# Dynamic convolution and tanh-shrink MLP: the load of the output weights is handed to the queue ahead of block 1's GpSimd products instead of behind two of them

## The chip, the cores and the metric

The kernel runs on one core of one Trainium2 chip. The metric is device time in microseconds (us) for one execution, and the median over runs is compared. The engines are named as in the profile: PE is TensorE's matmul, PEld its weight load, DVE is VectorE, ACT is ScalarE, POOL is GpSimd, SP is SyncE. SPq and POOLq are the instruction streams from which SP and POOL hand transfers to the 16 DMA engines; in the profile's list of DMA queues, q1 (hardware_dynamic) carries SP's transfers and q0 (software_dynamic) POOL's.

## The reference

Two steps. The first is a causal convolution over 7 positions whose weights differ for every token and head (softmax over the 7 taps); the second is a two-layer MLP with h - tanh(h) between.

```python
w = exp(weight_gen - max);  w = w / (sum(w) + 1e-09)        # B, S, 8 heads, 7 taps
x_pad = concatenate([zeros(B, 6, D), x], axis=1)            # B=8, S=4096, D=192
x_unf = x_pad[:, arange(S)[:, None] + arange(7)]            # B, S, 7, 192
y = einsum('bshk,bskhg->bshg', w, x_unf)                    # 24 channels a head
h = y.reshape(32768, 192) @ w_in                            # 192 x 2048
out = (h - tanh(h)) @ w_out                                 # 2048 x 192
```

## The kernel before

The 32,768 tokens are cut into 32 blocks of 1024. For each block the work goes through five stages.

1. SP loads x (with a halo of 6 earlier positions, into a ring of four places, `load_x`) and weight_gen (`load_wg`). ACT takes the exponential, DVE sums and scales.
2. The seven tap products, x times the tap's weight, are formed with `tap_product` (L299), in the steady state almost wholly on POOL. The products lie in the tiles `pa` (taps 0 to 3) and `pb` (taps 4 to 6). Some of them are added up by accumulating transfers that POOL issues (`dma_sum`, L288).
3. PE transposes the products with identity matmuls and adds the remaining ones up in PSUM (`conv_sums`, L526); ACT copies the result to `convT`.
4. The first matmul (`gemm1`, L586) makes 16 f tiles of 128 hidden channels from `convT` and `w_in`; for each, ACT forms tanh (L599) and DVE subtracts (L600) into `gt`. Three PSUM buffers rotate, so the matmul of f tile k waits for the subtraction of f tile k-3.
5. The second matmul (`out_stream`, L655) multiplies `gt` by `w_out`; ACT copies the result to `out_sb` (L674), and SP stores a whole block.

The instruction order on each engine is written out by hand; nothing reorders it. Each engine works through its own list, and waits stand where an operand has to be ready. In the steady state the second matmul of block n-1 runs between the f tiles of block n, and POOL forms the products of block n+2.

The change lies in the ramp, the first 37 us, where blocks 0 and 1 are prepared. Weights come in through POOL's queue, as these transfers also convert from fp32 to bf16. `load_w_in` (L747) brings f tiles 0 to 6 first, into the lower 64 partitions; ACT copies them to the upper 64 (L814). `rest_of_w_in` issues the second part, f tiles 7 to 15, behind block 0's last POOL product; as soon as it has landed, SP issues a transfer that copies it to the upper 64 partitions (L822). SP's queue then holds x of block 2 (L174) and a weight_gen tile (L163). `load_w_out` (L741) brings all of w_out. It is called from a hook in `products(1)`: the function goes through a list of tap products (engine, first tap, last tap plus one, token range) and calls a hook right behind the product whose first tap is the hook's key.

```python
TAPS1 = ((True, 0, 1, 0, 8), (True, 1, 2, 0, 8), (False, 4, 6, 0, 8), (False, 6, 7, 0, 8), (False, 2, 4, 0, 8))
...
        hooks={} if WOUT_CAST else {6: load_w_out},
```

`True` stands for DVE, `False` for POOL. With the key 6, POOL's list reads: second part of w_in, taps 4 and 5 of block 1 (one product), tap 6, w_out, taps 2 and 3, and then the first products of block 2, which wait for that block's x.

Of the kernel before, what the change touches and what calls it, by code (L numbers as in the profile page):

```python
# [16 lines left out]
def kernel(  # L17
# [61 lines left out]
    X3_BEHIND = None  # L79
    HALF = ()  # L80
    STORE_BEHIND = tuple(range(5, 31))
    WOUT_CAST = ()
    SKEW = 6
    TAPS1 = ((True, 0, 1, 0, 8), (True, 1, 2, 0, 8), (False, 4, 6, 0, 8), (False, 6, 7, 0, 8), (False, 2, 4, 0, 8))
# [57 lines left out]
    pace_of = {}  # L142
    sum_of = {}
    second = {}

    def order(inst, other, reason):
        tc.add_manual_dep(
            inst.ins,
            other.ins.name,
            mybir.DependencyInfo(mybir.DependencyClass.Sync, mybir.DependencyReason.DATA),  # L150
            reason=reason,
        )
# [3 lines left out]
    def tokens(t, n):  # L156

        m = n // 2
        return t[2 * m * TOK : 2 * (m + 1) * TOK].rearrange("(p s j) ... -> p s j ...", p=P, j=J)[:, n % 2]
# [127 lines left out]
    def dma_sum(out, in_):  # L287
        return nc.gpsimd.dma_start(  # L288
            out=out.rearrange("p k j d -> p k (j d)"),
            in_=in_.rearrange("p k j d -> p k (j d)"),  # L290
            accum_op=mybir.AluOpType.add,
            max_dma_last_dim=2 * J * D,
        )
# [65 lines left out]
    def products(n, taps=None, sums=None, hooks={}):  # L359
# [6 lines left out]
        pa = held[n][2] if n in held else papool.tile([P, KA, J, D], BF16, name="pa")  # L366
# [5 lines left out]
        else:  # L372
            if n in PB2:
                pb = npool.tile([P, K - KA, J, D], BF16, name="pb2", tag="spare")
            else:
                pb = pbpool.tile([P, K - KA, J, D], BF16, name="pb")
# [7 lines left out]
        def mul(eng, k0, k1, j0=0, j1=J):  # L384
            w = wsm_v if eng is nc.vector else wsm[:]
            return tap_product(eng, prod(k0, k1), x_t, w[:, j0:j1, :, k0:k1], (1, K), k0, k1, j0, j1)

        def parts(*ks):
            return [[prod(k, k + 1)[:, 0] for k in ks]] * NC
# [18 lines left out]
        def most(k0, k1):  # L408
            return mul(nc.gpsimd, k0, k1, 0, left[k0])
# [16 lines left out]
        def rest():  # L426
            a = PART_FILL.get(n, 0)
            if n in PART:
                if a:
                    mul(nc.gpsimd, KA, K, 0, a)  # L430
                dma_sum(pa[:, 0:2], pa[:, 2:4])
                if n + 1 in SCALE_EARLY:
                    prescale(n + 1)
            if n - 1 in whole:
                mul(nc.gpsimd, KA, K - 1)
                third_sum(n - 1)
                mul(nc.gpsimd, K - 1, K)
            else:
                mul(nc.gpsimd, KA, K, a, J)
            if n in PART:  # L440
                prods_of[n] = parts(4, 5, 6, 0, 1)
            else:
                def first_sum():
                    dma = dma_sum(pa[:, 0:3], pb[:, 0:3])
                    if n in LOCKED:
                        order(dma, last_sub[0], "place of the transfer")

                if n in LAST_TAP and n in SUM_BEHIND:
                    most(KA - 1, KA)
                    first_sum()  # L450
                elif n in SUM_LATE:
                    sum_of[n] = first_sum
                else:
                    a = min(FILL.get(n, 0), left[KA - 1]) if n in LAST_TAP else 0
                    if a:
                        mul(nc.gpsimd, KA - 1, KA, 0, a)
                    first_sum()
                    if n + 1 in SCALE_EARLY:
                        prescale(n + 1)
                    if n in LAST_TAP and a < left[KA - 1]:  # L460
                        mul(nc.gpsimd, KA - 1, KA, a, left[KA - 1])
                if n in TWO_SUMS:
                    to_sum[n] = pa
                    prods_of[n] = parts(0, 1)
                elif n in HALF:
                    to_sum[n] = pa
                    prods_of[n] = parts(3, 1, 0)
                else:
                    prods_of[n] = parts(3, 0, 1, 2)
                if n == NTOT - 1:  # L470
                    second_sum(n)
                    third_sum(n)
# [3 lines left out]
    def prescale(n):  # L476

        wsm, wsm_v, e_t, zr = wsm_of[n]
        scale(nc.gpsimd, wsm[:], e_t, zr[:])
        wsm_of[n] = (wsm, wsm_v, None, None)  # L480

    def second_sum(n):

        if n in to_sum:
            pa = to_sum.pop(n)
            pairs = 1 if n in HALF else 2
            second[n] = dma_sum(pa[:, 0:pairs], pa[:, 2 : 2 + pairs])
            if n in THREE or n in SINGLE:
                whole[n] = pa

    def third_sum(n):

        if n in whole:
            pa = whole[n]
            dma_sum(pa[:, 0:1], pa[:, 1:2])
            if n in SINGLE:
                whole.pop(n)
                prods_of[n] = [[pa[:, 0]]] * NC
# [142 lines left out]
    def out_stream():  # L641

        for i in range(LAST + 1):
            ops = []
            for r, blk in ((0, i), (1, i - 1)):
                if not 0 <= blk < LAST:
                    continue
                n, j = divmod(blk, J)
                if r == 0:
                    half[blk] = obank[blk % 2]  # L650
                ops.append((r, n, j, half[blk]))
            for f in range(NFT):
                for r, n, j, po in ops:
                    col = (j % 2) * HT + (j // 2) * P
                    mm = nc.tensor.matmul(  # L655
                        po[:, 0:D],
                        lhsT=g_of[n][f][r * R : (r + 1) * R, col : col + P],
                        rhs=w_out[r * R : (r + 1) * R, f, :],
                        start=(r == 0 and f == 0),
                        stop=(r == 1 and f == NFT - 1),  # L660
                    )
                    if r == 1 and f == 0 and i in (1, LAST):
                        order(mm, probe[0] if i == 1 else last_act[0], "row tiles in one bank")
                if f == NFT - 1 and i > 0:
                    store_out(i - 1)
                yield

    def store_out(blk):
        n, j = divmod(blk, J)
        po = half.pop(blk)  # L670
        if j == 0:
            out_of[n] = opool.tile([P, J, D], FP32, name="out_sb")
        out_sb = out_of[n]
        last_act[0] = nc.scalar.activation(out=out_sb[:, j, :], in_=po[:, 0:D], func=ACT.Copy)  # L674
        if j == J - 1:
            out_of.pop(n)
            g_of.pop(n)
            dma = nc.sync.dma_start(
                out=tokens(out, n),
                in_=out_sb[:],  # L680
            )
            if n in STORE_BEHIND and n + 3 in second:
                order(dma, second[n + 3], "order of the transfers")

    pairs = out_stream()

# [89 lines left out]
    def soft1():  # L776
# [17 lines left out]
        hooks={1: rest_of_w_in} | ({SOFT1_AT: soft1} if SOFT1_AT else {}),  # L794
# [24 lines left out]
    if SOFT_EARLY:  # L819
# [4 lines left out]
        1,  # L824
        taps=[(V if v else G_, k0, k1, j0, j1) for v, k0, k1, j0, j1 in TAPS1],
        sums=SUMS1,
        hooks={} if WOUT_CAST else {6: load_w_out},
    )
    conv(0, (0, 1), (2,))
    if not SOFT_EARLY:  # L830
# [200 lines left out]
```

## Time and profile before

| what | value |
|---|---|
| median of 3 runs | 735.81 us (735.81 to 737.36) |
| the profiled execution's own time | 735.9 us |
| its span, first to last instruction | 734.1 us |
| granted TensorE clock | 1.00 |
| PE busy | 715.7 us (97%) |
| DVE busy | 681.0 us (93%) |
| POOL busy | 660.6 us (90%) |
| ACT busy | 636.3 us (87%) |
| load of w_out, issue to landing | 9.9 us |
| second part of w_in, issue to landing | 5.2 us |

Times in the timelines are microseconds from the first instruction: start, length, engine, line, operation, output and inputs, count, and in brackets the idle time before it with what ended it. "w_out<-in_moe_w_out_dram" is a transfer by the names of its tiles. A DMA issue on SPq or POOL is the time in which the engine hands the transfer over; the transfer itself runs later. In the view by stretches the columns are length, busy time and count for PE, PEld, DVE, ACT, POOL, then the granted clock, the mean busy share of the 16 DMA engines and GB/s.

### The profile page before, as it was taken

How to read it: one execution, taken by the hardware profiler on the slowest of the kernel's cores; microseconds unless marked ns; L12 is line 12 of the kernel's file. 1: busy time of each engine (PE TensorE's matmuls, PEld its weight loads, DVE VectorE, ACT ScalarE, POOL GpSimd, SP SyncE). 2: the span in 40 equal slices, each digit the busy share in tenths (PEclk: the TensorE clock that was granted, in tenths of full speed). 3: DMA queues.
4: the chain of work that ended last, by engine and by line, in shares of the span. 5: the costliest groups of instructions: out<-in, count | busy, mean ns of one | idle time of the engine just before them, and what ended most of it. 6: DMA issues, size and time to landing. Idle time of an engine off the chain costs nothing.

```text
span 734.1 us, 29774 instructions
## 1 busy us (share of the span) xinstructions
PE 715.7 (97%) x13472; PEld 549.6 (75%) x13472; DVE 681.0 (93%) x718; ACT 636.3 (87%) x871; POOL 660.6 (90%) x170
## 2 busy tenths in 40 slices
PE   3899999999999999999999999999999999999998
PEld 2477877777777777777777777777777777777777
DVE  7999999999999999999999999999999999988883
ACT  4888888888889899999898998998998989888982
POOL 7999999999999999999999999999999999996000
PEclk9999999999999999999999999999999999999999
DMA  7745266664558787877888877787887878676412
GB/s 206 162 102 163 102 175 157 185 167 113 142 144 217 153 221 184 180 202 172 212 172 205 203 157 206 178 194 187 216 172 171 209 172 208 164 153 136 105 46 88
DMA packets 35053, 122.97 MB, mean 168 GB/s; under 512 B 4607, under 2 KB 9455, under 8 KB 33006
## 3 DMA queue, kind: packets, MB, share of 16 engines
q0 software_dynamic: 20208, 53.48, 42.4%
q1 hardware_dynamic: 14718, 67.59, 25.8%
q8 instruction: 105, 1.72, 0.9%
q14 instruction: 22, 0.18, 0.1%
HBM read 45.08 MB, written 25.17 MB: 96 GB/s over the span
## 4 chain that ended last, share of the span: by engine, by line
PE 94%; DVE 4%; ACT 1%; issue 0%; DMA 0%; DVEq 0%
PE obank L655 45%; PE ph L586 44%; PE pc L526 4%; DVE gt L600 2%; PE po L701 1%; DVE pa L299 1%; DVE pb L299 0%; DMA wg_t<-in_weight_gen_dram 0%; ACT th L599 0%; DVE obank L258 0%; DVE zsum L218 0%; DVE wsm L281 0%; ACT wg_t L204 0%; DVE obank L281 0%; ACT convT L544 0%
## 5 line engine op out<-in xcount | busy, mean ns | idle before, releaser
L600 DVE TENSOR_TENSOR gt<-ph,th 128x1024 bf16<-128x1024 f32 x512 | 598.6, 1218 | 32.2 <-ACT th L599 25.9
L599 ACT ACTIVATE th<-ph 128x1024 f32<-128x1024 f32 x512 | 513.0, 1027 | 65.5 <-PE ph L586 51.0
L586 PE MATMUL ph<-convT,w_in 64*128 64x512 bf16 x3072 | 412.9, 377 | 4.6 <-DVE gt L600 3.6
L655 PEld LDWEIGHTS <-gt 64*128 64x128 bf16 x7936 | 352.7, 94 | 84.4 <-issue 12.1
L655 PE MATMUL obank<-w_out,gt 64*128 64x192 bf16 x7936 | 405.9, 243 | 0.1
L299 POOL TENSOR_TENSOR pa<-x_ring,wsm 128x3072 bf16<-128x3072 f32 (+2 forms) x73 | 345.8, 5001 | 0.2
L299 POOL TENSOR_TENSOR pb<-x_ring,wsm 128x4608 bf16<-128x4608 f32 (+4 forms) x34 | 286.4, 8424 | 2.5 <-DMA pa<-pb 1.5
L586 PEld LDWEIGHTS <-w_in 64*128 64x128 bf16 x3072 | 158.9, 94 | 80.5 <-issue 12.9
L674 ACT ACTIVATE out_sb<-obank 128x192 f32<-128x192 f32 x248 | 81.7, 329 | 9.4 <-PE obank L655 8.2
L552 ACT ACTIVATE convT<-pc 128x1024 bf16<-128x1024 f32 (+1 forms) x62 | 50.8, 820 | 4.0 <-PE pc L526 3.8
L288 POOL DMA_DIRECT2D pa<-pa x24 | 39.7, 1656 | 8.6 <-DMA pa<-pb 8.3
L526 PEld LDWEIGHTS <-pa 64*128 64x128 bf16 x1920 | 39.7, 101 | 6.3 <-POOL pa L299 0.9
L288 POOL DMA_DIRECT2D pa<-pb x28 | 37.2, 1330 | 7.8 <-POOL pb L299 5.3
L526 PE MATMUL pc<-ident,pa 64*128 64x64 bf16 x1824 | 39.1, 192 | 1.3 <-POOL pa L299 0.8
L218 DVE TENSOR_REDUCE zsum<-wg_t 128x32 f32<-128x224 f32 (+1 forms) x61 | 23.7, 388 | 3.0 <-ACT wg_t L204 3.0
L204 ACT ACTIVATE wg_t<-wg_t 128x448 f32<-128x448 f32 x32 | 18.2, 569 | 6.6 <-DMA wg_t<-in_weight_gen_dram 6.6
L281 DVE TENSOR_TENSOR wsm<-wg_t,pc 128x448 f32<-128x448 f32 x27 | 16.8, 621 | 2.5
L299 DVE TENSOR_TENSOR pa<-x_ring,ph 128x384 bf16<-128x384 f32 x30 | 16.6, 554 | 1.3
L245 DVE RECIPROCAL pc<-zsum 128x64 f32<-128x64 f32 x27 | 14.8, 549 | 0.0
L526 PE MATMUL pc<-ident,pb 64*128 64x64 bf16 x216 | 4.9, 206 | 9.0 <-POOL pb L299 9.0
L526 PEld LDWEIGHTS <-pb 64*128 64x128 bf16 x288 | 6.3, 107 | 9.6 <-POOL pb L299 9.0
L701 PE MATMUL po<-w_out,gt 64*128 64x192 bf16 x256 | 11.9, 243 | 0.0
(26 smaller groups left out, 55.0 us busy)
## 6 DMA issues: line engine op xcount, KB each, us to landing
pa<-pb POOLq DMA_DIRECT2D x28, 1152.0 KB, 9.7
out_dram<-out_sb SPq DMA_DIRECT2D x31, 768.0 KB, 3.8
x_ring<-in_x_dram SPq DMA_DIRECT2D x15, 1344.0 KB, 8.1
pa<-pa POOLq DMA_DIRECT2D x24, 768.0 KB, 7.1
x_ring<-in_x_dram SPq DMA_DIRECT2D x17, 768.0 KB, 6.4
wg_t<-in_weight_gen_dram SPq DMA_DIRECT2D x32, 224.0 KB, 4.2
w_out<-in_moe_w_out_dram POOLq DMA_DIRECT2D x1, 768.0 KB, 9.9
out_dram<-out_sb SPq DMA_DIRECT2D x4, 192.0 KB, 3.4
```

The lines of the kernel that those rows point to most:

```text
L204: last_exp[0] = nc.scalar.activation(out=wg_t[:].rearrange("p j h k -> p (j h k)"), in_=wg_t[:].rearrange("p j h k -> p (j h k)"), func=AC ...
L218: nc.vector.reduce_sum(out=zsum_of[n][:, j0 * H : j1 * H], in_=e_of[n][:, j0:j1].rearrange("p j h k -> p (j h) k"), axis=AX.X,)
L288: return nc.gpsimd.dma_start(out=out.rearrange("p k j d -> p k (j d)"), in_=in_.rearrange("p k j d -> p k (j d)"), accum_op=mybir.AluOpTyp ...
L299: return eng.tensor_mul(bass.AP(tensor=out.tensor, offset=out.offset + j0 * D, ap=[out.ap[0], [J * D, nk], [G, run], [1, G]]), bass.AP(ten ...
L526: nc.tensor.matmul(pc[r][:, col : col + R] if home else pc[:, r, col : col + R], lhsT=prods[c][gi][r * R : (r + 1) * R, 2 * j : 2 * j + 2] ...
L552: last_conv[0] = nc.scalar.activation(out=out, in_=pc[:, :, 0:cols].rearrange("p r (cj t) -> p r cj t", t=R), func=ACT.Copy,)
L586: nc.tensor.matmul(ph[:, r, :], lhsT=w_in[r * R : (r + 1) * R, c, ff], rhs=convT[r * R : (r + 1) * R, c, :], start=(c == 0), stop=(c == NC ...
L599: last_act[0] = nc.scalar.activation(out=th[:], in_=ph_f, func=ACT.Tanh)
L600: last_sub[0] = nc.vector.tensor_sub(gt[:], ph_f, th[:])
L655: mm = nc.tensor.matmul(po[:, 0:D], lhsT=g_of[n][f][r * R : (r + 1) * R, col : col + P], rhs=w_out[r * R : (r + 1) * R, f, :], start=(r == ...
L674: last_act[0] = nc.scalar.activation(out=out_sb[:, j, :], in_=po[:, 0:D], func=ACT.Copy)
L701: nc.tensor.matmul(po[:, r, 0:D], lhsT=g_of[n][f][r * R : (r + 1) * R, col : col + P], rhs=w_out[r * R : (r + 1) * R, f, :], start=(f == 0 ...
```

## The change

The hook's key for `load_w_out` becomes a parameter, W_OUT_AT = 0. In block 1's list the product whose first tap is 0 is the first one, on DVE, so the call comes ahead of every POOL product of block 1. POOL's list then reads: second part of w_in, w_out, taps 4 and 5, tap 6, taps 2 and 3. The lists of PE, DVE, ACT and SP keep their order. A second parameter, STORE_BEHIND3, would let a store wait for another accumulating transfer; it is empty, and the waits of the stores are as they were.

```diff
+    STORE_BEHIND3 = ()
+    W_OUT_AT = 0
...
+    first_of = {}
...
-                    dma = dma_sum(pa[:, 0:3], pb[:, 0:3])
+                    dma = first_of[n] = dma_sum(pa[:, 0:3], pb[:, 0:3])
...
-            if n in STORE_BEHIND and n + 3 in second:
-                order(dma, second[n + 3], "order of the transfers")
+            before = second.get(n + 3) or (first_of.get(n + 3) if n in STORE_BEHIND3 else None)
+            if n in STORE_BEHIND and before is not None:
+                order(dma, before, "order of the transfers")
...
-        hooks={} if WOUT_CAST else {6: load_w_out},
+        hooks={W_OUT_AT: load_w_out},
```

## The prediction

> **What bounds the kernel now.** I read, in this order: the page's span and engine rows, busy time in three stretches, the chain of waits, the timelines of the three engines around the change, and the transfers.
>
> ```profile
> span 734.1 us, 29774 instructions
> 0.00:37.50 37.50, 22.53 (x438) 13.27 (x439) 32.90 (x37) 24.53 (x30) 32.85 (x17) 1.00 0.77 182
> 37.50:665.00 627.50, 627.42 (x11798) 483.26 (x11797) 597.08 (x634) 561.43 (x769) 618.04 (x152) 1.00 0.72 174
> 665.00:734.10 69.10, 65.74 (x1244) 53.06 (x1239) 51.05 (x49) 50.37 (x73) 9.69 (x3) 1.00 0.37 97
> ```
>
> The columns are stretch, length, then busy time (count) of PE, PEld, DVE, ACT, POOL, then granted clock, DMA share, GB/s. From 37.5 to 665 us PE is busy 627.42 of 627.50 us at clock 1.00: whatever ends the first 37.5 us later moves the end by as much, and hardly anything can be won behind it. The move happens inside that ramp, so the ramp has to be read next.
>
> ```profile
> 20.42 10.20 DVE gt L600 x9
> 30.65 0.84 PE ph L586 x6
> 31.52 0.83 ACT th L599
> 34.47 2.37 DVE gt L600 x2
> 36.88 0.82 PE ph L586 x6
> ```
>
> These are pieces of the chain (start, length). From 20.4 us the ramp is paced by DVE's subtractions of block 0 (1.13 us each); PE only waits for them. The gaps that the chain names "issue" between 20.4 and 37.7 us add up to 0.04+0.02+0.09+0.40+0.02+0.04 = 0.6 us.
>
> ```profile
> 14.66 0.67 POOL L747 DMA_DIRECT2D w_in<-in_moe_w_in_dram  x1
> 15.36 8.48 POOL L299 TENSOR_TENSOR pb<-x_ring,wsm 128x3072 bf16<-128x3072 f32 x2
> 23.79 1.20 POOL L741 DMA_DIRECT2D w_out<-in_moe_w_out_dram  x1
> 25.01 16.79 POOL L299 TENSOR_TENSOR pa<-x_ring,wsm 128x3072 bf16<-128x3072 f32 x3
> ...
> 19.93 0.72 SPq L822 DMA_DIRECT2D w_in<-w_in  x1
> 20.70 0.58 SPq L174 DMA_DIRECT2D x_ring<-in_x_dram  x1
> 21.46 1.44 SPq L163 DMA_DIRECT2D wg_t<-in_weight_gen_dram  x1
> ...
> 26.13 0.82 PE L586 MATMUL ph<-convT,w_in 64*128 64x512 bf16 x6 [0.31 <-DVE gt L600]
> 37.52 0.65 PE L655 MATMUL obank<-w_out,gt 64*128 64x192 bf16 x6
> ```
>
> POOL runs without a pause. The first reader of w_out starts at 37.52 us and waits for nothing; the load, issued at 23.79, lands 9.9 us later, at 33.6, with 3.9 us to spare. Three transfers on SP's queue are due while the moved load would now be under way: the copy of w_in's second part to the upper partitions (L822), read first by the PE group at 26.13 us (f tile 7), block 2's x (L174), and one weight_gen tile.
>
> ```profile
> 21.20:23.70 2.50, 1.65 (x12) 0.63 (x12) 2.50 (x3) 1.60 (x3) 2.50 (x1) 1.00 1.06 224
> 23.70:28.20 4.50, 3.41 (x45) 1.58 (x46) 4.50 (x5) 4.07 (x5) 4.48 (x3) 1.00 0.93 338
> 28.20:33.40 5.20, 4.89 (x135) 3.02 (x128) 5.20 (x6) 4.77 (x7) 5.20 (x2) 1.00 1.24 151
> ```
>
> The DMA engines work through the copy (to 23.7), then x and weights (to 28.2), then w_out (to 33.4).
>
> **The change, part by part.**
>
> *The program.* The instruction orders of PE, DVE, ACT and SP are unchanged. On POOL one issue moves: it now stands right behind the issue of w_in's second part and ahead of the two-tap product and the one-tap product of block 1 (the products keep their own order). The name says "body 0"; the code does it in block 1's products. STORE_BEHIND3 is empty, so the store's order is as before.
>
> *POOL.* Nothing is added: the issue's 1.20 us goes from 23.79 to about 15.36. The two products of 8.48 us in sum start 1.20 us later and end at 25.01, where the issue ended before. Their readers are transposes of block 1 whose first POOL tap is used at 28.37 us on PE; the two-tap product now ends near 22.2 instead of 21.0, the other near 25.0 instead of 23.8, read at 31.3 or later. Covered by over 3 us: cost 0. If that issue takes as long as the longest kind of POOL issue in the page (1656 ns mean, the in-place sums), POOL is 0.46 us late from 25.0 on; block 2's last product then ends at 51.0 to 51.5 plus 0.46, and PE reads it at 52.17: still covered, 0. Below zero: the POOL total does not fall, so no gain.
>
> *The load itself.* Landing earlier is worth 0, since its only reader has 3.9 us of slack already.
>
> *What it now stands in front of.* This is the only price. w_in's second part moves from 16.05 us; by the trace's packet records its 16 engines finish it between 18.4 and 19.6 us. w_out is 2064 packets, 129 on each engine, that start 31.7 ns apart on an engine: 128 x 31.7 ns = 4.06 us. Queued directly behind w_in it ends, engine by engine, between 22.5 and 23.65 us. The copy's first packets started at 21.30 before. If an engine finishes what it was given first, the copy starts 1.2 to 2.35 us later. Two rows decide whether it does:
>
> ```profile
> q0 software_dynamic: 211, 0.65, 107.8%
> ...
> q0 software_dynamic: 79, 0.24, 52.9%
> q1 hardware_dynamic: 79, 0.49, 50.0%
> ```
>
> The first is the transfers' view of 66 to 69.4 us: SP had issued a store at 65.80, and only POOL's queue q0 moves until its sum is nearly through. The other two are 159 to 161.5 us: a store issued at 154.44 waits about four microseconds and then shares evenly. So: first come first served, for a few microseconds at least. I take that, as w_out has only some 2 us left at 21.3.
>
> Copy: landed at 24.09 us by the semaphore records; plus 2.35 on the worst engine, 26.44. PE wants it at 26.13, and DVE's subtraction of that tile starts 0.24 us after its tanh is done (28.26 against 28.01), so 0.31 - 0.24 = 0.07 us reaches the chain; on the mean engine (plus 1.8) none.
>
> x of block 2: landed at 28.23; plus 2.35, 30.58. POOL reads it from 30.59 us. Cost 0, with no slack left on the worst engine. Should POOL wait some tenths, block 2's products end by 51.5 plus that, and PE takes them at 52.17.
>
> weight_gen: landed at 28.77, read by the exponential at 44.92. Cost 0. SP's next load (36.25 us) waits for POOL's first product of block 2 and moves only with it.
>
> Upper bound of this price: w_out does not start before w_in has landed (19.91) and takes from first to last packet what it took before (27.63 to 33.36, 5.7 us), ending at 25.6; the copy then takes its 21.30 to 24.09 = 2.8 us, landing at 28.4: 2.3 late, less 0.24, that is 2.1 us on the chain. x would land near 32.5, 1.9 us late for POOL; PE, itself 2.1 us late, would find block 2's products in time. So 0 to 2.1 us; I take 0.1, as the back-to-back packet spacing is a measured row of this very transfer, while the bound adds a second start-up that one queue's neighbours need not have. Lower bound 0: the readers' start is set by DVE, not by these transfers; the 0.6 us of chain gaps is all that could shrink at most.
>
> The Trainium skill ("DMA: Bandwidth & Descriptors", section "Queues, rings and completion order") says that an engine round-robins between the queue rows that have work, packet by packet. The 159 us row agrees, the 66 us row does not for its 3.4 us. By that rule the copy would share with w_out's last 2 us instead of standing behind it, an estimate of about 1 us late, landing near 25.1: still ahead of 26.13, so the sum would be 0.0 instead of 0.1.
>
> **Sum.** 0 (POOL) + 0 (w_out's reader) + 0.1 (copy) + 0 (x) = +0.1 us. The profiled execution took 735.9 us, 1.8 more than its span of 734.1, and 0.1 above the median of 735.81; on the median this gives 735.9.
>
> **Rivals.**
>
> *The copy is held up for longer (slower).* Place: PE's f tile 7 at 26.13 us waits for L822. It decides once the copy lands later than 26.37 us (26.13 + 0.24), and beyond 0.2% (1.5 us) once it lands later than 27.9. For it: SP's transfers get behind one that is already handed out (the 66 us row); w_out's packets are as small as 384 bytes, and its slowest engine ended 0.8 us behind the second slowest (33.34 against 32.51). Against it: most engines are free by 23.6. Price up to 2.1 us: 737.9.
>
> *An earlier w_out frees something (faster).* The 28.2 to 33.4 us stretch has no w_out traffic any more. For it: DVE's and PE's path runs right through it, and 0.6 us of gaps lie in the chain. Against: DVE's subtractions take 1.13 us each both before and during w_out's traffic, and PE is full from 37.5 on. Price at most -0.6 us: 735.2; more than 0.2% faster would need something that the trace does not show.
>
> *The load is hidden altogether*: copy and x land in time by sharing or by luck of the engines; 735.8, which is inside "no change".
>
> **How the numbers follow.** 0.2% of 735.8 is 1.5 us, which is also the spread of the runs shown (735.81 to 737.36) and about what a measurement of this kernel can tell from no change. Hidden or nearly so (0 to 1.4 us, and gaps that shrink): 0.58. Slower by more than 1.5 us: 0.34, since two transfers end up with no slack at all in my sum, so that each microsecond that I have too little counts in full, and POOL's delay could add to PE's. Faster by more than 0.2%: 0.08. Range: from 735.2 (gaps gone) to 737.9 (the bound), widened by 0.2 below for a run's scatter and 0.4 above for a wait of POOL on x that outlasts PE's.
>
> **What the changed profile would show.** POOL's issue of w_out near 15.4 us, its products ending near 25.0, the 28.2 to 33.4 us stretch with little DMA traffic. Right: the copy lands before 26.4 and the subtractions run on at 1.13 us through 28.3 us, with no POOL gap at 30.6. Wrong: a PE gap at f tile 7 put down to the copy, a gap of POOL before its product at 30.6 us, PE waits for POOL near 52 us, or the issue on POOL taking far longer than 1.2 us.

## The result, and the profile after

The changed kernel is slower: 739.62 us median (739.39 to 741.10) against 736.61 us before (735.81 to 737.36) measured beside it, a ratio of 1.0045 with a 95% interval of 1.0032 to 1.0058. Measured twice more, on two chips, it was 1.0033 (1.0023 to 1.0043) and 1.0041 (1.0026 to 1.0056). The forecast was 735.9, no change, with a range up to 738.3. It was built on the median of the first three runs of the kernel before, 735.81; the six runs beside the changed kernel gave 736.61, so 0.8 us of the 3.7 us between forecast and measurement is the base; the change itself is 3.0 us, where 0.1 was forecast.

First the page's span and the view by stretches of the changed kernel (length, then busy time and count of PE, PEld, DVE, ACT, POOL, granted clock, DMA share, GB/s):

```profile
span 737.5 us, 29774 instructions
37.50:41.00 3.50, 2.90 (x74) 1.79 (x74) 3.26 (x4) 3.50 (x6) 3.50 (x1) 1.00 0.71 242
41.00:665.00 624.00, 623.91 (x11745) 481.29 (x11743) 593.50 (x631) 558.57 (x765) 612.99 (x151) 1.00 0.72 174
```

From 41.0 us on PE is as full as it was from 37.5 on before. All of the 3.4 us are lost ahead of that point. The chain of the ramp (start, length) names what it was:

```profile
14.95 6.06 DMA w_in<-in_moe_w_in_dram
21.03 7.64 DMA w_in<-w_in
28.72 2.17 PE ph L589 x11
```

Up to 28.7 us the chain no longer runs through DVE's subtractions but through two transfers: the load of w_in's second part and its copy to the upper partitions (line numbers are some 3 or 4 higher in this kernel). The timelines of PE, DVE and POOL show the same from the readers' side:

```profile
26.72 0.37 PE L589 MATMUL ph<-convT,w_in 64*128 64x512 bf16 x1 [0.42 <-DVE gt L603]
28.72 2.54 PE L589 MATMUL ph<-convT,w_in 64*128 64x512 bf16 x11 [1.62 <-DMA w_in<-w_in]
41.04 0.65 PE L658 MATMUL obank<-w_out,gt 64*128 64x192 bf16 x6
...
31.07 2.51 DVE L603 TENSOR_TENSOR gt<-ph,th 128x1024 bf16<-128x1024 f32 x2 [1.99 <-ACT th L602]
...
15.61 1.20 POOL L745 DMA_DIRECT2D w_out<-in_moe_w_out_dram  x1
16.83 8.49 POOL L302 TENSOR_TENSOR pb<-x_ring,wsm 128x3072 bf16<-128x3072 f32 x2
25.29 5.62 POOL L302 TENSOR_TENSOR pa<-x_ring,wsm 128x3072 bf16<-128x3072 f32 x1
31.77 11.21 POOL L302 TENSOR_TENSOR pa<-x_ring,wsm 128x3072 bf16<-128x3072 f32 x2 [0.87 <-DMA x_ring<-in_x_dram]
```

One matmul of f tile 7 (which reads the lower partitions) runs at 26.72; the next one needs the copy and waits until 28.72. DVE's eighth subtraction starts at 31.07 instead of 28.26, the first matmul with w_out at 41.04 instead of 37.52. POOL's list is as forecast up to 30.9, then it waits 0.87 us for block 2's x.

The way of the copy, in both profiled executions (landings by the semaphore records, packets by the packet records):

| event, us | before | after | later by |
|---|---|---|---|
| w_in's second part issued | 14.66 | 14.95 | 0.29 |
| it lands | 19.91 | 21.01 | 1.10 |
| copy issued | 19.93 | 21.03 | 1.10 |
| w_out's last packet, first to last engine | 31.9 to 33.4 | 23.6 to 25.7 | other place |
| copy's packets, first start to last end | 21.30 to 23.75 | 23.55 to 27.68 | 2.25 to 3.93 |
| copy landed | 24.09 | 28.67 | 4.58 |
| block 2's x landed | 28.23 | 31.64 | 3.41 |

The copy's first packet starts at 23.55 us, when the first engine has finished w_out (23.56). Of the 4.58 us, 0.29 lie in a later start of POOL's products ahead of the change (8.96 and 9.24 us), which differs from execution to execution, 0.81 in the load of w_in (6.06 instead of 5.25 us), and 3.48 between the copy's issue and its landing (7.64 instead of 4.16).

There is one more loss that I had not priced. In this execution the clock falls behind PE's wait:

```profile
26.80:28.70 1.90, 0.29 (x1) 0.00 (x0) 1.90 (x2) 0.81 (x1) 1.90 (x1) 1.00 1.00 304
28.70:30.00 1.30, 1.28 (x8) 0.55 (x10) 0.38 (x1) 0.00 (x0) 1.30 (x1) 0.60 1.00 419
30.00:32.40 2.40, 2.40 (x55) 1.76 (x53) 1.28 (x2) 2.05 (x2) 1.53 (x2) 0.51 0.41 158
```

PE is busy for 0.29 of 1.90 us, and then works at a granted clock of 0.60 and 0.51 until 32.4 us, where the kernel before has 1.00 from 20.2 us on.

### The profile page after: what moved, and what is told of

Same layout as the page of the kernel before. It is cut to its first block, busy times and chain, and to the rows that moved or that the text cites. A ratio compares the mean times of both kernels' runs of the same rounds, so it can differ in the third digit from the quotient of the medians.

```text
span 737.5 us, 29774 instructions
## 1 busy us (share of the span) xinstructions
PE 718.6 (97%) x13472; PEld 552.3 (75%) x13472; DVE 681.4 (92%) x718; ACT 636.0 (86%) x871; POOL 660.6 (90%) x170
## 4 chain that ended last, share of the span: by engine, by line
PE 94%; DMA 2%; POOL 1%; ACT 1%; issue 1%; DVE 1%; POOLq 0%; DVEq 0%; ACTq 0%
PE obank L658 45%; PE ph L589 44%; PE pc L529 4%; PE po L705 1%; DMA w_in<-w_in 1%; DMA w_in<-in_moe_w_in_dram 1%; POOL pa L302 1%; ACT th L602 0%; DMA wg_t<-in_weight_gen_dram 0%; DVE gt L603 0%; POOL pb L302 0%; PE obank L529 0%; ACT wg_t L207 0%; ACT convT L547 0%; DVE zsum L221 0%
## 5 line engine op out<-in xcount | busy, mean ns | idle before, releaser
L603 DVE TENSOR_TENSOR gt<-ph,th 128x1024 bf16<-128x1024 f32 x512 | 598.9, 1217 | 35.3 <-ACT th L602 28.5
L589 PEld LDWEIGHTS <-w_in 64*128 64x128 bf16 x3072 | 160.9, 95 | 81.2 <-issue 12.2
L221 DVE TENSOR_REDUCE zsum<-wg_t 128x32 f32<-128x224 f32 (+1 forms) x61 | 23.6, 387 | 3.0 <-ACT wg_t L207 3.0
```

Of the source, the lines that this page charges most:

```text
L221: nc.vector.reduce_sum(out=zsum_of[n][:, j0 * H : j1 * H], in_=e_of[n][:, j0:j1].rearrange("p j h k -> p (j h) k"), axis=AX.X,)
L589: nc.tensor.matmul(ph[:, r, :], lhsT=w_in[r * R : (r + 1) * R, c, ff], rhs=convT[r * R : (r + 1) * R, c, :], start=(c == 0), stop=(c == NC ...
L603: last_sub[0] = nc.vector.tensor_sub(gt[:], ph_f, th[:])
```

## The experiments

The theory (called Q in the expectations): the copy stands behind w_out in the DMA engines, f tile 7 waits for it, and the ramp is late by that wait. Its first rival (P): the early issue costs through POOL or through w_in's load, whatever stands behind it. Its second rival: the clock.

### Half of w_out in front

```diff
-    def load_w_out():
...
+    def load_w_out(c0=0, c1=NFT):
...
-        hooks={W_OUT_AT: load_w_out},
+        hooks={0: lambda: load_w_out(0, 8), 6: lambda: load_w_out(8, NFT)},
```

> The first half of w_out (8 of 16 row groups) is issued at the new place, the second half at the old place. Theory Q (the copy of w_in's second part stands in the DMA engines behind every byte of w_out, and f tile 7 waits for it): half the bytes in front, so the copy lands about 2.3 us later than before instead of 4.6, near 26.4 us, just when it is needed; 736.6 to 737.4 us. Rival P (the early issue holds up POOL and w_in's second part itself, whatever its size): one early issue is still there, about as slow as the changed kernel, 738.5 to 739.6.

Measured: 736.45 us, ratio to before 0.9994 (0.9985 to 1.0002). The copy landed at 25.08 us, earlier than the 26.4 expected, and PE did not wait for it. The rival P falls: an early issue alone costs nothing. w_in's load took 6.2 us here too, so that slowing alone costs nothing either.

### w_out behind block 1's two-tap product

```diff
-    W_OUT_AT = 0
+    W_OUT_AT = 4
```

> w_out is issued behind block 1's two-tap product and ahead of its one-tap product (hook key 4), at about 21 us, when the copy and block 2's x have been handed out. Theory Q: w_out's bytes come behind the copy and x, so the copy lands near 24 us as before; no change against the kernel before, 736.0 to 737.3. Rival P (any place ahead of a product of block 1 costs, through the late products): half of the loss stays, 738 or more.

Measured: 736.51 us, ratio 0.9994 (0.9985 to 1.0003). In the profiled execution w_in's load took 5.3 us again, the copy 4.5 us from its issue to its landing, and f tile 7 waited only for DVE. What matters is whether the copy has been handed out first, not which product w_out passes.

### One and a half times the bytes

```diff
     def load_w_out():
         nc.gpsimd.dma_start(out=w_out[:], in_=moe_w_out.rearrange("(c p) e -> p c e", c=NFT))
+        spare = npool.tile([P, NFT // 2, D], BF16, name="spare", tag="spare")
+        nc.gpsimd.dma_start(
+            out=spare[:], in_=moe_w_out.rearrange("(c p) e -> p c e", c=NFT)[:, : NFT // 2]
+        )
```

> The changed kernel with a second issue behind w_out that loads half of w_out again into a tile that nobody reads: 1.5 times the bytes in front of the copy. Theory Q: copy lands 2 to 2.5 us later than in the changed kernel, and every microsecond of that reaches the end: 741.5 to 742.5. Rival P: one more issue of 1.2 us on POOL, hidden or at most 1.2 more: 739.6 to 740.8. If the clock alone were the cause: 739.6.

Measured: 739.25 us, ratio 1.0035 (1.0024 to 1.0047): no more than the changed kernel loses. Here the theory as I had put it, that the copy waits for every byte in front of it, falls. The chain and the transfers of this kernel in two stretches, 21 to 24.9 and 26 to 31 us, show why (packets, MB, share of the 16 engines):

```profile
20.87 7.85 DMA w_in<-w_in
```

```profile
q0 software_dynamic: 1873, 0.71, 154.6%
...
q1 hardware_dynamic: 259, 1.62, 95.5%
q0 software_dynamic: 242, 0.09, 15.1%
```

For about four microseconds behind the copy's issue only POOL's queue moves; the copy's first packet starts at 25.10 us. From then on the two queues take turns packet by packet, 259 against 242 in the second stretch; as a packet of POOL's load has 384 bytes and one of SP's 2,304 (the copy) or 10,752 (x), SP gets nearly all of the time, and the additional bytes cost nothing more: some 700 of POOL's 3,072 packets of data start only after the copy's first. So the copy does not wait for all that lies in the other queue, and the wait looks bounded in time: 4.2 us from the issue to the first packet here, 4.4 in the kernel with w_out 3 us later (below), and 4.35 for the store that the prediction shows (issued at 154.44, first packet at 158.79), while some 127, 83 and 16 packets an engine passed on POOL's queue. What sets this bound the traces don't show.

In the rows of 159 to 161.5 us that the prediction shows the turns are visible in the same way, 79 packets against 79. The Trainium skill ("DMA: Bandwidth & Descriptors", section "Queues, rings and completion order") states this round-robin by packets; the traces agree with it for the second part of such a meeting and not for its first four microseconds.

### PE kept busy during the wait

```diff
         ff = slice(f * P, (f + 1) * P)
+        if n == 0 and f == 7:
+            for _ in range(10):
+                nc.tensor.matmul(
+                    ph[:, 0, :], lhsT=w_in[0:R, 0, 0:P], rhs=convT[0:R, 0, :], start=True, stop=True
+                )
```

> The changed kernel with ten extra matmuls of w_in against convT ahead of f tile 7, into the PSUM tile that f tile 7 then overwrites: PE stays busy while the copy is awaited. Theory Q with a share for the clock: the copy lands as late as in the changed kernel (near 28.7 us), but the half clock that the changed kernel shows from 29.0 to 32.4 us does not come, worth about 0.9 us: 738.4 to 739.0. If the clock were all of it: 736.6 to 737.2. If the clock were worth nothing: 739.6 or a little more.

Measured: 738.48 us, ratio 1.0026 (1.0017 to 1.0035). In its profiled execution the extra matmuls run from 26.05 to 28.37 us, f tile 7 follows at 28.21, overlapping the last of them, without a wait, and the clock stays at 1.00 from 20.3 us on. It was run again next to the changed kernel on one chip:

> The ten extra matmuls ahead of f tile 7 again, next to the changed kernel. If the half clock after PE's wait is a part of the loss: 0.6 to 1.2 us less than the changed kernel on this chip. If it isn't: the same.

> The changed kernel once more, on the same chip as the next one: 739.2 to 739.9.

Measured there: 738.60 us, ratio 1.0034 (1.0022 to 1.0046), against 738.33 us, ratio 1.0041 (1.0026 to 1.0056), for the changed kernel. The pair shows no difference, and the changed kernel came out below what I had expected. So a share of the clock in the median isn't shown. The clock does show between executions of the changed kernel itself:

> The changed kernel again on this chip, as the control of the others: 739.2 to 740.0. Its profile tells whether the half clock from 29.0 to 32.4 us comes in each execution: if PE's wait of 2 us always brings it, a stretch at clock 0.5 follows the wait again; if it depends on where the wait falls in the clock's own steps of 3.4 us, it may be missing and the span be about 1 us shorter.

Measured: 739.35 us, ratio 1.0033 (1.0023 to 1.0043). In its profiled execution PE waits as well, but the half clock does not follow:

```profile
span 736.5 us, 29774 instructions
28.48 1.47 PE L589 MATMUL ph<-convT,w_in 64*128 64x512 bf16 x11 [1.30 <-DMA w_in<-w_in]
28.50:30.00 1.50, 1.50 (x30) 0.86 (x32) 0.67 (x1) 0.66 (x1) 1.50 (x1) 1.00 0.95 398
39.67 0.65 PE L658 MATMUL obank<-w_out,gt 64*128 64x192 bf16 x6
```

The same eleven matmuls take 1.47 us instead of 2.54, and the span is 736.5 us; 736.6 in the third profiled execution, also without a half clock. Against the profiled execution of before (734.1 us of span, one of its fastest) that is 2.4 us, and about 1 us more where the half clock comes; the first matmul with w_out is 2.15 and 2.48 us late in the two executions without it and 3.52 in the one with it. The stretches of half clock in the records last 3.4 us or a multiple (28.96 to 32.38 us in the first execution). The Trainium skill ("TensorE: Matmul & The Clock Gate", section "What's actually happening") describes a free-running window of 3.4 us; the trace agrees on this length. Counted on in steps of 3.413 us from the changes of clock in the records, PE's wait lies almost wholly within one step in all three executions. What differs is how long PE was busy in that step: 1.36 of 3.41 us ahead of the half clock (25.55 to 28.96), 1.90 and 1.82 us in the other two (26.07 to 29.48 and 27.22 to 30.63). A sharp border isn't shown: 1.73 us was followed by half clock in the kernel with the late copy (24.17 to 27.59, below), and 1.65 us was not in the kernel with the extra matmuls (20.30 to 23.71).

### w_out 3 us later, behind a single-tap product

```diff
-    W_OUT_AT = 0
+    W_OUT_AT = 4
...
-    TAPS1 = ((True, 0, 1, 0, 8), (True, 1, 2, 0, 8), (False, 4, 6, 0, 8), (False, 6, 7, 0, 8), (False, 2, 4, 0, 8))
+    TAPS1 = ((True, 0, 1, 0, 8), (True, 1, 2, 0, 8), (False, 4, 5, 0, 8), (False, 5, 6, 0, 8), (False, 6, 7, 0, 8), (False, 2, 4, 0, 8))
```

> Block 1's two-tap product on POOL is cut into two one-tap products and w_out is issued between them, near 18.2 us: w_in's second part has by then moved for 2 us, and w_out is handed out about 2 us before the copy. In the changed kernel, the halved one and the one with more bytes w_in's second part took 6.0 to 6.2 us from issue to landing, against 5.2 to 5.3 with w_out issued later. If the copy's wait in the engines is the cause whatever happens to w_in: w_in lands after 5.3 us again, the copy is issued about 0.8 us earlier than in the changed kernel, still stands behind w_out and lands near 27.5 to 28; 738.0 to 739.0 us. If the slowed w_in were the main cause: 736.4 to 737.2.

Measured: 741.82 us, ratio 1.0071 (1.0058 to 1.0083), worse than expected and worse than the changed kernel. Its chain, its PE timeline and its clock:

```profile
14.66 5.29 DMA w_in<-in_moe_w_in_dram
19.97 9.73 DMA w_in<-w_in
```

```profile
29.74 2.74 PE L589 MATMUL ph<-convT,w_in 64*128 64x512 bf16 x11 [2.61 <-DMA w_in<-w_in]
28.80:35.50 6.70, 5.76 (x84) 3.80 (x86) 2.67 (x3) 2.48 (x3) 4.46 (x2) 0.50 0.55 189
```

w_in's load is on time (5.29 us) and the copy is issued at 19.97, as before; w_out had been issued at 18.21 and its first packet starts at 20.13, just behind the copy's issue. The copy then takes 9.73 us. In the profiled execution two steps of half clock follow. That w_in's load is slowed by a follower in its queue is therefore not what costs; the copy's own wait is. It is longer here than in the changed kernel (9.73 against 7.64 us) mostly ahead of the first packet, which starts 4.4 us after the issue (24.34) instead of 2.5; from there to the last packet it takes 4.4 us instead of 4.1. Why the wait is longer I did not separate.

### The copy taken out

```diff
-    def load_w_in(c0, c1, f0, f1, behind=None):
+    def load_w_in(c0, c1, f0, f1, behind=None, p0=0):
...
     def rest_of_w_in():
         load_w_in(0, NC, FA, F)
+        load_w_in(0, NC, FA, F, p0=R)
...
-    nc.sync.dma_start(out=w_in[R:P, :, FA:F], in_=w_in[0:R, :, FA:F])
```

The second load goes straight from DRAM into the upper partitions (p0=R).

> The copy to the upper partitions is taken out: POOL issues a second converting load of w_in's second part straight into the upper 64 partitions, behind the first and ahead of w_out, which keeps the new place (hook key 0). Nothing that f tile 7 needs stands behind w_out now. If the copy's wait is the whole cause: w_in's upper part lands near 23, f tile 7 starts on time, and the time is that of the same kernel with hook key 6, 736.5 to 737.5. If block 2's x (late behind w_out, POOL waits for it near 31 us) or POOL's later products cost as well: 738 or more.

> The same without the copy, and with w_out at the old place (hook key 6). The control for the run before: by either theory as fast as the kernel before, 736.3 to 737.3; if POOL's added issue of 0.7 us delays block 2's products past 52 us, up to 0.7 more.

Measured: 736.71 us with w_out at the new place, ratio 0.9998 (0.9989 to 1.0007), and 736.74 us at the old place, ratio 1.0003 (0.9994 to 1.0012). Without the copy the early w_out costs nothing. PE and DVE of the first of the two run through:

```profile
26.71 0.82 PE L589 MATMUL ph<-convT,w_in 64*128 64x512 bf16 x6 [0.46 <-DVE gt L603]
24.15 10.44 DVE L603 TENSOR_TENSOR gt<-ph,th 128x1024 bf16<-128x1024 f32 x9 [0.35 <-ACT th L602]
```

One thing limits this pair: SP, which no longer waits for w_in, loads block 2's x earlier too (landed at 19.65 us), so it doesn't test a late x.

### The copy late, w_out at its old place

The kernel before, with one edit; x of block 2 goes ahead of the copy.

```diff
-    nc.sync.dma_start(out=w_in[R:P, :, FA:F], in_=w_in[0:R, :, FA:F])
...
+        if f == 2:
+            copy = nc.sync.dma_start(out=w_in[R:P, :, FA:F], in_=w_in[0:R, :, FA:F])
+            order(copy, last_sub[0], "late copy")
```

> The kernel before, with w_out at its old place; only the copy of w_in's second part waits until DVE's third subtraction of block 0 is done (near 23.8 us) instead of until w_in has landed (19.9). Block 2's x, which stood behind the copy, goes ahead of it and is early. If the late copy is by itself the cause: it lands near 28 us (1.4 to 4.1 us to its first packets and about 2.8 to land, w_out's packets being handed out at the same moment), some 1.7 us after 26.4: 738.0 to 739.5. If the loss needs w_out ahead of x, or POOL's late products: 736.3 to 737.3.

Measured: 738.96 us, ratio 1.0039 (1.0026 to 1.0052), the changed kernel's loss with w_out unmoved. The chain and the PE timeline:

```profile
23.86 4.50 DMA w_in<-w_in
```

```profile
28.40 2.74 PE L586 MATMUL ph<-convT,w_in 64*128 64x512 bf16 x11 [1.88 <-DMA w_in<-w_in]
```

The copy lands at 28.35 us, and f tile 7 waits 1.88 us. (The profiled execution, 740.66 us, is the slowest of the five; two steps of half clock follow the wait in it.) A late copy is thus enough for the loss. In the pair before, which has no copy (and an early x), the loss is gone.

### Block 2's x late, no copy

The kernel without the copy and with w_out at the new place; x of block 2 waits for a POOL product of block 1.

```diff
+    pool_tap = {}
...
+                pool_tap[n, k0] = m
...
-    load_x(2)
+    load_x(2, pool_tap[1, 6])
```

> The kernel without the copy (w_out at the new place), in which x of block 2 was loaded early because SP no longer waited for w_in. Here that load waits until block 1's one-tap product on POOL is done (near 26 us) and then stands behind w_out: x lands near 31.5 to 33, and POOL's first product of block 2 starts 0 to 1.5 us late, as in the changed kernel, while f tile 7 is on time. If the late copy is the whole cause of the loss: POOL's delay is covered by the 0.7 to 1.2 us ahead of PE's first transpose of block 2 near 52 us, 736.4 to 737.4. If late x costs by itself: 737.4 to 738.5.

Measured: 738.19 us, ratio 1.0025 (1.0014 to 1.0036). A late x costs by itself, against the first expectation. POOL and PE:

```profile
33.34 11.20 POOL L303 TENSOR_TENSOR pa<-x_ring,wsm 128x3072 bf16<-128x3072 f32 x2 [1.62 <-DMA x_ring<-in_x_dram]
53.75 1.39 POOL L285 TENSOR_TENSOR wsm<-wg_t,zr 128x448 f32<-128x448 f32 x1
54.27 0.88 PE L531 MATMUL pc<-ident,pb 64*128 64x64 bf16 x48 [1.15 <-POOL pb L303]
```

POOL starts block 2 at 33.34 us here, 2.75 us later than in the kernel before, and PE waits 1.15 us for its last product. (The median is 1.7 us above the 736.48 of before; what makes up the rest is not separated.) PE starts 0.52 us behind POOL's following instruction (54.27 and 53.75). Before, that instruction stood at 51.00 and PE came at 52.17, so the slack was about 52.17 - 51.52 = 0.65 us, not more. In the changed kernel POOL starts block 2 at 31.77, 1.18 us late, and its instruction stands at 52.18; PE, itself late through the copy, comes at 55.69 and waits for nothing. There the late x is hidden behind the larger loss. With the copy on time it would have been worth about 1.18 - 0.65 = 0.5 us; this last number is worked out, not measured.

## Why the prediction was wrong

**The step that failed** is the copy's: "plus 2.35 on the worst engine, 26.44", of which 0.07 us was to reach the chain. It landed at 28.67. The 2.35 came from w_in's end on the last engine (19.6) and 4.06 us of w_out's packets, 23.65. Measured on the last engine to finish: w_in ended at 20.7 and w_out at 25.7, 2.1 us later than I had it. Somewhat more than half of this is w_in, 1.14 us late: 0.27 us is its later first packet, the rest its load, which took 6.0 to 6.2 us from issue to landing wherever w_out was issued directly behind it and 5.25 to 5.29 us in the kernel before and in the two kernels with the hook key 4; I had taken it as unchanged without a reason. The rest, 0.94 us, is w_out: its packets did not keep the pace of the old place (between 20.5 and 24.0 us POOL's queue moved 71 to 97 KB in half a microsecond, against 86 to 97 between 28.5 and 32.0 at the old place). From there the copy took its 3 us.

**The slower rival was right** in its place (f tile 7 waiting for L822), its point of decision (a landing behind 26.4 us) and, by its bound, in its size: it took w_out's end at 25.6 and the landing at 28.4, against 25.7 and 28.7. That these ends agree so closely is partly luck: the bound let w_out begin behind w_in's landing, at 19.91, and take 5.7 us; it began at 19.33, before w_in had landed (21.01), and took 6.4. I had given the rival 0.34, and the sum 0.1 instead of something between 0.1 and 2.1 us. A sum that leaves two transfers without any slack on the worst engine was no case for taking the cheap end.

**What the bound lacked** is the clock: its 2.1 us came as 2.15 and 2.48 us at the first matmul with w_out without a half clock and as 3.52 with it, and the range ended at 738.3. How much of the median is clock isn't shown. The base of 735.81, 0.8 us under the median of the six runs, put the whole range low by as much; even with 736.61 it would have ended at 739.1, below the 739.62 measured.

**Right:** POOL (the two products ended at 25.3, the issue took 1.20 us, nothing of it reached the end), w_out's early landing worth nothing, PE full behind the ramp so that the loss passes on in full, and no gain from the quieter stretch. **Wrong besides:** x of block 2 was to land at 30.58 and cost 0; it landed at 31.64 and, by the working above, alone would have cost about half a microsecond, as the cover ahead of 52.17 us was 0.65 us.

**The two rows on the queues** were read half right. "First come first served, for a few microseconds at least" is what the traces show; but it is a bounded wait, and in the kernel with one and a half times the bytes the copy landed at 28.71 us, against 28.67 in the changed kernel. Turns from the first packet on would have put the landing near 25.1 us by the prediction's estimate.

## What to carry to other kernels

Moving a load earlier is not free because its reader has slack: list every transfer that will be handed out while it moves, and give each its slack on the slowest engine, with a start-up for the load moved. Where a wait is left without slack, take the upper bound, and allow for the clock that PE may lose behind a stop of some 2 us. Small loads for a paced reader belong in front of a large one, or must not need a second hop: here the load of w_in straight into both halves made the place of w_out indifferent.

## What the runs showed of the hardware that was not expected

- A transfer that SP issues while POOL's queue is busy gets its first packet later than the 1.4 us of the kernel before: after 2.5 to 2.7 us in the three executions of the changed kernel, when the first engine had finished the load ahead, and after 4.2 to 4.4 us where POOL's queue had work for longer. Then the two queues take equal turns by packets, whatever their sizes (259 against 242, 79 against 79).
- A load is slowed by another load issued right behind it on the same queue: 6.0 to 6.2 us instead of 5.25 to 5.29, also when the follower has half the size. It is late already when the first engine finishes it (4.25 us after the issue instead of 3.77), before the follower's first packet starts (19.33 us in the changed kernel).
- A stop of PE of 1.3 to 1.7 us brought half clock for 3.4 us in one execution of the changed kernel and none in two others; the spans differ by 1 us. PE had been busy for 1.36 us of the step of 3.41 us that holds the stop in the first, 1.90 and 1.82 us in the others.
